# Feed-forward jobs beside attention in one group of sixteen pairs instead of two of eight

## The chip, the cores and the metric

The kernel runs on one core of one Trainium2 chip. The core has a matrix engine (TensorE, PE in the profile, its weight loads PEld), a vector engine (DVE), a scalar engine (ACT), a general one (POOL), and SP, which issues DMAs. Matmuls write to PSUM, eight banks of 128 partitions x 512 f32; ACT and DVE read it from there. The metric is the device time of one execution in microseconds: 1838.07 us as median of three runs before the change (1837.73 to 1839.37).

## What is computed

One transformer block over 2048 tokens of width 512, all in f32: a modulated layer norm, attention with 32 heads of 16, a residual, a second modulated layer norm, a gated feed-forward part of width 1792, a residual.

```python
mod = (_silu(c) @ w_mod).reshape(1, 6, 1, -1)
sa, ca, ga, sb, cb, gb = (mod[:, i] for i in range(6))
h = _layernorm(x) * (1 + ca) + sa
qkv = (h @ wqkv).reshape(B, S, 3, 32, 16)           # q, k, v: [heads, S, 16]
p = _softmax(einsum("bhqd,bhkd->bhqk", q, k) * 16 ** -0.5)
x = x + ga * (einsum("bhqk,bhkd->bhqd", p, v) @ wo)
h = _layernorm(x) * (1 + cb) + sb
x = x + gb * ((_silu(h @ w_gate) * (h @ w_up)) @ w_down)
```

## The kernel before

**Precision.** An f32 product is formed as three products of a high and a low part (terms (0,0), (0,1), (1,0) of hi and lo). Scores are made with 48 rows: 16 head rows in three such combinations stacked on the partitions, two heads of a group on rows 0 to 63 and 64 to 127; two further rows (KR = 48, KR + 1) carry the negated row maximum.

**Units, steps, pairs.** The queries are cut into four chunks of 512 (NC), the heads into eight groups of four (NG). A unit u is one chunk with one group, 32 in all. A unit has 16 steps, one for each 128 keys; a step has four pairs. A pair (`pair_of`) is one score matmul (`score`, L568, 128 keys x 512 queries of one head) on one half of the array's rows, and beside it on the other half one matmul for row maxima (`max_one`, L521), 20 steps ahead (LEAD - 1) of the scores. ACT turns each score bank into exps (L570) in a tile `pt_`, of which there are 13 (PTS). DVE reduces each bank of the maxima (L523). For the last 80 pairs there are no maxima left. `done` counts pairs up to 4n = 2048.

**pv.** `pv_step(i, half)` multiplies the four exp tiles of step i with v, for half the queries: eight PE instructions (L583) of 32 array columns and 256 elements, two quads. They run as four column tiles side by side and add to one bank for the whole unit. Behind the last step ACT copies the bank to o (L587), and `close_unit` issues the DMA of the denominators, the loads of k and q of unit u + 3 and, some steps later through `at`, the reciprocal (L598), the load of the broadcast reciprocals rb, and on POOL o times rb (L610) with its store. `pvs(most, by_halves)` issues up to `most` halves whose step lies at least 8 pairs back (`4 * halves[0][0] + 8 <= done`).

**Two ways to go on.** `plain(steps)` goes in windows of three pairs, each followed by one or two halves of pv, with four banks for maxima (0 to 3), three for scores (4 to 6) and bank 7 for pv. `filled(places, work)` runs feed-forward work beside the pairs: after pair r it takes `places[r]` slots of the work, then come `hook()` and `pvs(6, False)`. The maxima have banks 0, 1, 2 there, the scores 4 and 5, the work accumulates in banks 3 and 6 (`outs`, FBANKS), pv in 7. In the last 80 pairs ALONE replaces the places, and the scores have five banks.

**Feed-forward work.** After a chunk's eight units its output projection (`out_pair`, two jobs of two row tiles), gate and up products (`gate_up`, 14 jobs, f = 0 to 13) and down products (`down`, 14 jobs, two for each m = 0 to 6) run beside the next chunk's attention. In `accumulate` with `halves` a slot is two matmuls of 64 rows, one on each half of the array, one to each of the two `outs`: in phase 0 outs[0] gets the upper 64 rows and outs[1] the lower, in phase 1 the other way round. A `gate_up` or `out_pair` job has 12 slots a phase, 24 in all, a `down` job 6 and 12. The chunk's jobs come in the order gate 0, 1, 2, down (0, 0), (0, 2), gate 3, 4, down (1, 0), (1, 2), and so on to gate 13 and down (6, 0), (6, 2). In the main loop an `out_pair` or `gate_up` job goes in two calls of `filled` with TWO, one phase each, with a block of pv between; a `down` job in one call with DOWN. Between the phases of a `down` job `read_both` lets ACT copy one element of each of the two banks (L878), so that the second phase's matmuls wait until the first phase has landed.

After its last slot a `gate_up` job issues the tanh on ACT (L835), and in `hook` follow q and m32 on DVE (L839, L841) and the split of m32 into `mid` on POOL (L843, L844). A `down` job adds its two banks to x on DVE (L855) right after its last slot. `out_pair` leaves two additions (L803) to `hook` and the sums for the norm (L807, L808) to `side`, from which each pair takes one entry. `max_turned` puts a unit's negated maxima into the rows KR of q: a small reduce m, a scaling on ACT, two small DVE instructions and eight DMAs on SP.

**Order.** All engines run their instructions in the order in which the program issues them (`tc.manual_schedule()`); waits between engines follow from the tiles. `gate_up` asks on SP for the next job's weights (`wgu`, two tiles of 1 MB); `down` for the next `wd` after its second job. The main loop for each of the first three chunks: `plain` up to step STARTS (147, 275, 403), two `out_pair` jobs, `plain(9)`, `plain(3)` with the transposes of the normalised rows, in the third chunk `plain(24)`, then the jobs (all 28, in the third chunk 21; the rest runs after the attention). Before the last couple of down jobs stands `plain(3)`.

Of the kernel before, what the change touches and what calls it, by code (L numbers as in the profile page):

```python
# [19 lines left out]
P = 128  # L20
# [23 lines left out]
PTS = 13  # L44
FBANKS = (3, 6)
# [4 lines left out]
TWO = (0, 3, 2, 2, 2, 2, 1, 0)  # L50
DOWN = (0, 3, 3, 0, 3, 3, 0, 0)
ALONE = {TWO: (0, 4, 0, 4, 0, 4, 0, 0), DOWN: (0, 6, 0, 0, 0, 6, 0, 0)}

# [48 lines left out]
def block_kernel(ctx, tc, x, wqkv, wo, w_gate, w_up, w_down, c, w_mod, out):  # L102
# [391 lines left out]
    posts = []  # L494
    n = 16 * NU
# [66 lines left out]
    def score(i, h):  # L562
        u, kt = divmod(i, 16)
        rows = slice(64 * (h % 2), 64 * (h % 2) + KR + 2)
        p_ = pb.tile([P, CW], F32, name="pt_", tag="pt", bufs=PTS)
        pts.setdefault(i, {})[h] = p_
        sp = bank("st_")
        nc.tensor.matmul(sp, kop[u % 3][rows, h // 2, kt * P:(kt + 1) * P], qop[u][rows, h // 2, :],  # L568
                         start=True, stop=True)
        nc.scalar.activation(p_, sp, AF.Exp, scale=SCALE)  # L570

    def pv_step(i, half):

        u, kt = divmod(i, 16)
        g = u % NG
        cols = slice(half * HQ, (half + 1) * HQ)
        if kt == 0 and half == 0:
            pv[u] = single("pv")
            o_[u] = pf.tile([P, CW], F32, name="o", tag="o", bufs=2)
        p_ = pts.pop(i) if half else pts[i]  # L580
        for h in range(4):
            e0 = (kt * H + 4 * g + h) * (DH + 1)
            nc.tensor.matmul(pv[u][32 * h:32 * h + 32, cols], v_flat[:, e0:e0 + 32], p_[h][:, cols],  # L583
                             start=(kt == 0 and half == 0), stop=(kt == 15),
                             skip_group_check=half == 1)
        if kt == 15 and half:
            nc.scalar.copy(o_[u], pv[u])  # L587
# [19 lines left out]
    def out_c(u, eng, mul, o, rb):  # L607
        ci, g = divmod(u, NG)
        on = pf.tile([P, CW], F32, name="on", tag="on", bufs=1)
        mul.tensor_mul(on, o, rb)  # L610
        eng.dma_start(o_dr[ci, g], on)
# [204 lines left out]
    def out_pair(ch, t0, outs, halves):  # L816
        return accumulate(outs, lambda e, a, k: ch.oT[a][:, k, (t0 + e) * P:(t0 + e + 1) * P],
                          lambda b, k: ch.wo[k // 2][:, b, k % 2, :], NK,
                          lambda: posts.append(lambda: add_o(ch, t0, outs, True)), halves)
# [7 lines left out]
    def gate_up(ch, f, outs, halves):  # L827
# [5 lines left out]
        def after():  # L833
            th = tmp("th")
            nc.scalar.activation(th, outs[0], AF.Tanh, scale=0.5)  # L835

            def later():
# [11 lines left out]
                          halves)  # L849
# [85 lines left out]
    def after(i):  # L935
# [9 lines left out]
        if i == -2:  # L945
# [4 lines left out]
            kop[2] = pf.tile([P, 2, S], F32R, name="kop2")  # L950
            ones_rows(2)
# [44 lines left out]
    def pvs(most, by_halves):  # L996
# [4 lines left out]
        while most and halves and 4 * halves[0][0] + 8 <= done:  # L1001
# [30 lines left out]
    def filled(places, work):  # L1032
# [3 lines left out]
        four, bank = three, Turn(4, 5)  # L1036
        if done >= 4 * n - 4 * (LEAD - 1):
            places, bank = ALONE.get(places, places), Turn(4, 5, 0, 1, 2)
        for r in range(len(places)):
            pair_of()  # L1040
            take(work, places[r])
            if r % 4 == 3:
                end_steps()
        hook()
        pvs(6, False)
# [14 lines left out]
    for ci in range(last):  # L1060
        plain(STARTS[ci] - done // 4)
        ch = chunks[ci]
        for t0 in (0, 2):
            work = out_pair(ch, t0, outs, True)
            filled(TWO, work)
            filled(TWO, work)
# [5 lines left out]
        for _ in range(len(ch.jobs) - (KEEP if ci == last - 1 else 0)):  # L1072
# [3 lines left out]
            work = job(ch, *args, outs, True)  # L1076
            for places in (TWO, TWO) if job is gate_up else (DOWN,):
                filled(places, work)
# [80 lines left out]
```

## Time and profile before

| | us |
|---|---|
| median of three runs | 1838.07 |
| lowest, highest | 1837.73, 1839.37 |
| the profiled execution | 1838.88 |
| its span, first to last instruction | 1837.1 |
| PE busy in it | 1825.5 |
| DVE busy | 1532.5 |
| ACT busy | 1243.7 |
| POOL busy | 460.4 |

The granted clock of TensorE is 1.000 over the whole span. The profile's page gives busy time by engine, and by line with the count, the mean time of one instruction, and the idle time before it with what ended it. PE's matmuls are pipelined, so that a PE that reads as busy can still run at different paces; its pace is read from the starts of its matmuls in the timeline. A row of the timeline gives the start in us from the span's start, the length, the engine, the line, the operation, what it writes and reads, the form, and how many like ones in a row are merged.

### The profile page before, as it was taken

How to read it: one execution, taken by the hardware profiler on the slowest of the kernel's cores; microseconds unless marked ns; L12 is line 12 of the kernel's file. 1: busy time of each engine (PE TensorE's matmuls, PEld its weight loads, DVE VectorE, ACT ScalarE, POOL GpSimd, SP SyncE). 2: the span in 40 equal slices, each digit the busy share in tenths (PEclk: the TensorE clock that was granted, in tenths of full speed). 3: DMA queues.
4: the chain of work that ended last, by engine and by line, in shares of the span. 5: the costliest groups of instructions: out<-in, count | busy, mean ns of one | idle time of the engine just before them, and what ended most of it. 6: DMA issues, size and time to landing. Idle time of an engine off the chain costs nothing.

```text
span 1837.1 us, 41048 instructions
## 1 busy us (share of the span) xinstructions
PE 1825.5 (99%) x16904; PEld 1198.2 (65%) x16904; DVE 1532.5 (83%) x2578; ACT 1243.7 (68%) x2386; POOL 460.4 (25%) x541
## 2 busy tenths in 40 slices
PE   9999999999999999999999999999999999999999
PEld 7876444444455777776565777776564577777887
DVE  5578999999999888889999888889999988831544
ACT  4223888888877777777878777777878877774211
POOL 3612544565223111111123111111123011130200
PEclk9999999999999999999999999999999999999999
DMA  8884876657845444453544554444643545333642
GB/s 305 286 225 149 183 185 199 168 189 178 209 79 125 102 120 141 118 147 70 149 103 105 134 132 116 123 117 90 158 81 57 111 93 149 138 122 121 271 169 110
DMA packets 80488, 267.63 MB, mean 146 GB/s; under 512 B 19604, under 2 KB 24212, under 8 KB 59620
## 3 DMA queue, kind: packets, MB, share of 16 engines
q1 hardware_dynamic: 61324, 179.71, 33.8%
q0 software_dynamic: 18288, 84.49, 19.3%
q8 instruction: 133, 2.18, 0.5%
q10 hardware_dynamic: 688, 0.80, 0.2%
q14 instruction: 55, 0.45, 0.1%
HBM read 201.85 MB, written 62.13 MB: 144 GB/s over the span
## 4 chain that ended last, share of the span: by engine, by line
PE 96%; DVE 2%; ACT 1%; DMA 1%; SPq 0%; issue 0%; DVEq 0%
PE bank L583 27%; PE bank L781 19%; PE bank L568 18%; PE bank L521 14%; PE bank L791 8%; PE bank L211 7%; DVE mx L523 1%; PE bank L824 1%; DMA wm_ab<-in_w_mod 1%; PE bank L765 0%; DVE stt L807 0%; PE bank L533 0%; PE bank L163 0%; PE bank L534 0%; PE bank L535 0%
## 5 line engine op out<-in xcount | busy, mean ns | idle before, releaser
L523 DVE TENSOR_REDUCE mx<-bank 128x1 f32<-128x512 f32 x2048 | 1276.0, 681 | 108.5 <-PE bank L521 66.2
L568 PE MATMUL bank<-qop,kop 50*128 50x512 f32 x2048 | 730.2, 425 | 1.0 <-ACT pt__16517 L570 0.2
L521 PE MATMUL bank<-kop,qop 48*128 48x512 f32 x2048 | 726.6, 425 | 2.9 <-DVE mx L523 2.6
L568 PEld LDWEIGHTS bank<-qop,kop 50*128 50x128 f32 x2048 | 342.6, 184 | 169.9 <-issue 55.6
L521 PEld LDWEIGHTS bank<-kop,qop 48*128 48x128 f32 x2048 | 343.5, 184 | 113.9 <-DVE mx L523 67.7
L781 PE MATMUL bank<-act,wgu 64*128 64x512 f32 x1872 | 300.9, 392 | 0.0
L781 PEld LDWEIGHTS bank<-act,wgu 64*128 64x128 f32 x1872 | 196.1, 187 | 24.7 <-issue 0.2
L610 POOL TENSOR_TENSOR on<-o,rb 128x512 f32<-128x512 f32 x31 | 39.8, 1284 | 498.1 <-DMA rb<-d_dr 363.6
L781 PE MATMUL bank<-wd,mid 64*128 64x512 f32 x912 | 134.0, 397 | 0.0
L843 POOL CAST mid<-m 128x512 fp32r<-128x512 f32 x40 | 24.3, 608 | 379.3 <-DVE m L841 176.5
L781 PEld LDWEIGHTS bank<-wd,mid 64*128 64x128 f32 x912 | 88.0, 185 | 15.9 <-ACT first L878 3.2
L211 PE MATMUL bank<-hT,wqs 128*128 128x512 f32 x384 | 94.3, 397 | 0.4 <-DVE wqs L351 0.4
L839 DVE SCALAR_TENSOR_TENSOR q<-th,bank 128x512 f32<-128x512 f32 x56 | 38.2, 682 | 54.4 <-ACT th L835 54.4
L211 PEld LDWEIGHTS bank<-hT,wqs 128*128 128x128 f32 x384 | 70.7, 188 | 18.8 <-issue 2.9
L835 ACT ACTIVATE th<-bank 128x512 f32<-128x512 f32 x56 | 33.3, 594 | 58.1 <-PE bank L791 58.1
L855 DVE TENSOR_TENSOR x<-bank,x 128x512 f32<-128x512 f32 x84 | 53.9, 685 | 18.3 <-PE bank L781 16.8
L841 DVE TENSOR_TENSOR m<-bank,q 128x512 f32<-128x512 f32 x56 | 38.7, 691 | 21.7 <-PE bank L791 19.7
L844 POOL TENSOR_TENSOR mid<-m,mid 128x512 fp32r<-128x512 f32 x40 | 51.5, 1287 | 3.3
L791 PE MATMUL bank<-wd,mid 128*128 128x512 f32 x216 | 51.4, 393 | 0.0
L211 PE MATMUL bank<-wqs,hT 128*128 128x512 f32 x192 | 48.0, 398 | 0.0
L781 PE MATMUL bank<-wgu,act 64*128 64x512 f32 x288 | 47.8, 394 | 0.1
L791 PEld LDWEIGHTS bank<-wd,mid 128*128 128x128 f32 x216 | 40.3, 188 | 9.1 <-POOL mid L844 0.3
(6298 smaller groups left out, 5133.0 us busy)
## 6 DMA issues: line engine op xcount, KB each, us to landing
wgu<-gu_dr SPq DMA_DIRECT2D x48, 1024.0 KB
wd<-wd_dr SPq DMA_DIRECT2D x28, 1024.0 KB
kop<-kd SPq DMA_DIRECT2D x33, 768.0 KB
kop<-kd POOLq DMA_DIRECT2D x29, 768.0 KB, 8.8
gu_dr<-wgu POOLq DMA_DIRECT2D x14, 1024.0 KB, 13.5
kd<-prt SPq DMA_DIRECT2D x16, 512.0 KB
qd<-prt SPq DMA_DIRECT2D x16, 512.0 KB
kop<-gu_dr SPq DMA_DIRECT2D x8, 1024.0 KB
```

The costliest lines, as they stand in the source:

```text
L211: nc.tensor.matmul(pt, lhs(a, k), rhs(b, k), start=(n == 0), stop=(n == 3 * nk - 1))
L521: nc.tensor.matmul(pm, qop[u][rows, s, qt * P:(qt + 1) * P], kop[u % 3][rows, s, kc * CW:(kc + 1) * CW], start=True, stop=True)
L523: nc.vector.tensor_reduce(mx[u][:, b, s, qt, kc:kc + 1], pm, op=ALU.max, axis=AX.X)
L568: nc.tensor.matmul(sp, kop[u % 3][rows, h // 2, kt * P:(kt + 1) * P], qop[u][rows, h // 2, :], start=True, stop=True)
L583: nc.tensor.matmul(pv[u][32 * h:32 * h + 32, cols], v_flat[:, e0:e0 + 32], p_[h][:, cols], start=(kt == 0 and half == 0), stop=(kt == 15), ...
L610: mul.tensor_mul(on, o, rb)
L781: nc.tensor.matmul(outs[e], lhs(e, a, k)[rows], rhs(b, k)[rows], start=(ph == 0 and j == 0), stop=(j == z and (ph == 1 or trade is not None)),
L791: nc.tensor.matmul(outs[e], lhs(e, a, k), rhs(b, k), start=(j == 0), stop=(j == z))
L839: nc.vector.scalar_tensor_tensor(q, th, 1.0, outs[0], op0=ALU.add, op1=ALU.mult)
L841: nc.vector.tensor_mul(m32, outs[1], q)
L844: (nc.gpsimd if slow else nc.vector).tensor_sub(mid[:, 1, :], m32, mid[:, 0, :].bitcast(F32))
L855: nc.vector.tensor_add(ch.x2[:, t, :], outs[e], ch.x2[:, t, :])
```

## The change

A gate, up or out job now runs in one call of `filled` with FOUR, 16 pairs with 24 slots, and one block of up to ten halves behind it, drawn with a lag of four pairs. As both phases lie in one group, `read_both` stands between them (`trade`). The second down job of a couple has places of its own and the lag of four as well. A group of 16 pairs holds 16 exps, so four exp tiles are added (MORE, in the pool `pf`), the tiles go round in a list (`ring`) that the program keeps itself, and where 17 wouldn't do up to four halves are drawn before a group. Space for the tiles comes from o (one buffer, taken only at the unit's end) and from rb (the product with o is written in place). Where a unit's pv begins beside other work, bank 7 trades places with the next bank of the maxima. The tanh of a gate job moves into `hook`. In the last 80 pairs a FOUR job runs as two groups of eight as before.

```diff
@@ -42,14 +42,15 @@
 ORDER = (0, 2, 1, 3)
 UG = 16 * NG
 PTS = 13
+MORE = 4
 FBANKS = (3, 6)
 KEEP = 7
 REST = 24
 NORM = 9
 STARTS = (147, 275, 403)
-TWO = (0, 3, 2, 2, 2, 2, 1, 0)
-DOWN = (0, 3, 3, 0, 3, 3, 0, 0)
-ALONE = {TWO: (0, 4, 0, 4, 0, 4, 0, 0), DOWN: (0, 6, 0, 0, 0, 6, 0, 0)}
+FOUR = (1, 2, 1, 2, 2, 1, 3, 0, 3, 1, 2, 1, 2, 1, 2, 0)
+DOWN = ((0, 3, 3, 0, 3, 3, 0, 0), (0, 3, 3, 0, 2, 1, 1, 2))
+ALONE = {FOUR: (0, 4, 0, 4, 0, 4, 0, 0), DOWN[0]: (0, 6, 0, 0, 0, 6, 0, 0), DOWN[1]: (0, 6, 0, 0, 0, 6, 0, 0)}
 
 
 def run(it):
@@ -492,6 +493,7 @@
     pf = None
     qop, mx, pts, pv, o_, due, res = {}, {}, {}, {}, {}, {}, {}
     posts = []
+    ring = [pb.tile([P, CW], F32, name=f"pt{k}", bufs=1) for k in range(PTS)]
     n = 16 * NU
     last = NC - 1
 
@@ -562,7 +564,8 @@
     def score(i, h):
         u, kt = divmod(i, 16)
         rows = slice(64 * (h % 2), 64 * (h % 2) + KR + 2)
-        p_ = pb.tile([P, CW], F32, name="pt_", tag="pt", bufs=PTS)
+        p_ = ring.pop(0)
+        ring.append(p_)
         pts.setdefault(i, {})[h] = p_
         sp = bank("st_")
         nc.tensor.matmul(sp, kop[u % 3][rows, h // 2, kt * P:(kt + 1) * P], qop[u][rows, h // 2, :],
@@ -575,8 +578,10 @@
         g = u % NG
         cols = slice(half * HQ, (half + 1) * HQ)
         if kt == 0 and half == 0:
+            if beside and u and done < 4 * n - 4 * (LEAD - 1):
+                j = three.ids[three.n % len(three.ids)]
+                banks[7], banks[j] = banks[j], banks[7]
             pv[u] = single("pv")
-            o_[u] = pf.tile([P, CW], F32, name="o", tag="o", bufs=2)
         p_ = pts.pop(i) if half else pts[i]
         for h in range(4):
             e0 = (kt * H + 4 * g + h) * (DH + 1)
@@ -584,6 +589,7 @@
                              start=(kt == 0 and half == 0), stop=(kt == 15),
                              skip_group_check=half == 1)
         if kt == 15 and half:
+            o_[u] = pf.tile([P, CW], F32, name="o", tag="o", bufs=1)
             nc.scalar.copy(o_[u], pv[u])
 
 
@@ -606,9 +612,8 @@
 
     def out_c(u, eng, mul, o, rb):
         ci, g = divmod(u, NG)
-        on = pf.tile([P, CW], F32, name="on", tag="on", bufs=1)
-        mul.tensor_mul(on, o, rb)
-        eng.dma_start(o_dr[ci, g], on)
+        mul.tensor_mul(rb, o, rb)
+        eng.dma_start(o_dr[ci, g], rb)
 
     def at(i, f):
         due.setdefault(i, []).append(f)
@@ -816,7 +821,7 @@
     def out_pair(ch, t0, outs, halves):
         return accumulate(outs, lambda e, a, k: ch.oT[a][:, k, (t0 + e) * P:(t0 + e + 1) * P],
                           lambda b, k: ch.wo[k // 2][:, b, k % 2, :], NK,
-                          lambda: posts.append(lambda: add_o(ch, t0, outs, True)), halves)
+                          lambda: posts.append(lambda: add_o(ch, t0, outs, True)), halves, trade=halves and read_both)
 
     def out_terms(ch, t, pt, ks):
         for k in ks:
@@ -831,10 +836,15 @@
         ch.mid[f] = mid = tile_mid()
 
         def after():
-            th = tmp("th")
-            nc.scalar.activation(th, outs[0], AF.Tanh, scale=0.5)
-
-            def later():
+            def half():
+                th = tmp("th")
+                nc.scalar.activation(th, outs[0], AF.Tanh, scale=0.5)
+                return th
+
+            th = None if halves else half()
+
+            def later(th=th):
+                th = th or half()
                 q = tmp("q")
                 nc.vector.scalar_tensor_tensor(q, th, 1.0, outs[0], op0=ALU.add, op1=ALU.mult)
                 m32 = tmp("m32")
@@ -846,7 +856,7 @@
 
         w = ch.w.pop(f)
         return accumulate(outs, lambda e, a, k: w[:, 2 * e + a, k, :], lambda b, k: ch.hT[b][:, k, :], NK, after,
-                          halves)
+                          halves, trade=halves and read_both)
 
     def down(ch, m, t0, outs, halves):
         def later():
@@ -948,6 +958,7 @@
             es_a0.close()
             pf = ctx.enter_context(tc.tile_pool(name="pf", bufs=1, side="right", reuse_waits="tile"))
             kop[2] = pf.tile([P, 2, S], F32R, name="kop2")
+            ring[:0] = [pf.tile([P, CW], F32, name=f"pt{PTS + k}") for k in range(MORE)]
             ones_rows(2)
             load_k(2)
             load_q(2)
@@ -993,12 +1004,12 @@
         while side:
             side.pop(0)()
 
-    def pvs(most, by_halves):
+    def pvs(most, by_halves, lag=8):
 
         nonlocal owed
         if by_halves:
             most, owed = most + owed, 0
-        while most and halves and 4 * halves[0][0] + 8 <= done:
+        while most and halves and 4 * halves[0][0] + lag <= done:
             i, half = halves.pop(0)
             pv_step(i, half)
             most -= 1
@@ -1034,15 +1045,23 @@
         nonlocal four, bank, beside
         beside = True
         four, bank = three, Turn(4, 5)
+        lag = 4 if len(places) == 16 or places == DOWN[1] else 8
+        twice = 1
         if done >= 4 * n - 4 * (LEAD - 1):
+            twice, lag = len(places) // 8 or 1, 8
             places, bank = ALONE.get(places, places), Turn(4, 5, 0, 1, 2)
-        for r in range(len(places)):
-            pair_of()
-            take(work, places[r])
-            if r % 4 == 3:
-                end_steps()
-        hook()
-        pvs(6, False)
+        if done - 4 * halves[0][0] + len(places) > PTS + MORE:
+            pvs(4, False, 4)
+        for k in range(twice):
+            if k:
+                bank = Turn(4, 5, 0, 1, 2)
+            for r in range(len(places)):
+                pair_of()
+                take(work, places[r])
+                if r % 4 == 3:
+                    end_steps()
+            hook()
+            pvs(6 if len(places) < 16 else 10, False, lag)
 
     def two_of(u):
         return [kop[u % 3][:, e, :].rearrange("p (k c) -> p k c", k=NK) for e in range(2)]
@@ -1061,9 +1080,7 @@
         plain(STARTS[ci] - done // 4)
         ch = chunks[ci]
         for t0 in (0, 2):
-            work = out_pair(ch, t0, outs, True)
-            filled(TWO, work)
-            filled(TWO, work)
+            filled(FOUR, out_pair(ch, t0, outs, True))
         side.append(lambda: scaled(ch))
         plain(NORM)
         plain(WIN, [lambda tp, k=k: ch.turned(tp, k) for k in range(NK)])
@@ -1073,9 +1090,7 @@
             job, args = ch.jobs.pop(0)
             if args == (NF // FG - 1, 0):
                 plain(WIN)
-            work = job(ch, *args, outs, True)
-            for places in (TWO, TWO) if job is gate_up else (DOWN,):
-                filled(places, work)
+            filled(FOUR if job is gate_up else DOWN[args[1] // 2], job(ch, *args, outs, True))
     chunks[last - 1].load_gu(NF - 2)
     filled((0,) * 4, iter(()))
 
```

## The prediction

> **What bounds the kernel now.** I read the page first, then the groups by line, the busy time of two stretches, and last the timelines of TensorE, VectorE and ScalarE through one stage.
>
> ```profile
> span 1837.1 us, 41048 instructions
> PE 1825.5 (99%) x16904; PEld 1198.2 (65%) x16904; DVE 1532.5 (83%) x2578; ACT 1243.7 (68%) x2386; POOL 460.4 (25%) x541
> L523 DVE TENSOR_REDUCE mx<-bank 128x1 f32<-128x512 f32 x2048 | 1276.0, 681 | 108.5 <-PE bank L521 66.2 <-PE bank L568 34.1
> 300.00:371.40 71.40, 71.40 (x716) 34.41 (x712) 70.73 (x122) 61.54 (x123) 34.88 (x35) 1.00 0.70 194
> 646.90:687.70 40.80, 40.80 (x438) 29.96 (x434) 36.40 (x61) 29.19 (x56) 6.85 (x8) 1.00 0.48 125
> ```
>
> The last two rows give a stretch's length, then the busy time of PE, PEld, DVE, ACT and POOL, each with its instructions. PE reads as busy everywhere, so it doesn't say who bounds. DVE does: in the plain stretch (300 to 371 us) it has work for 70.73 of 71.40 us; beside the other matmuls (646.9 to 687.7 us: four TWO groups and two DOWN groups) it is idle for 4.4 of 40.8 us. So there are two regimes. Plain is paced by the maxima's reduces:
>
> ```profile
> 864.19 0.50 PE L568 MATMUL bank<-qop,kop 50*128 50x512 f32 x1
> 864.76 3.68 DVE L523 TENSOR_REDUCE mx<-bank 128x1 f32<-128x512 f32 x6 [0.20 <-PE bank L568]
> 868.36 0.24 DVE L598 RECIPROCAL dn<-dn 128x16 f32<-128x16 f32 x1
> 868.51 5.63 DVE L523 TENSOR_REDUCE mx<-bank 128x1 f32<-128x512 f32 x9
> 886.05 14.56 DVE L523 TENSOR_REDUCE mx<-bank 128x1 f32<-128x512 f32 x24 [0.25 <-PE bank L521]
> ```
>
> 24 reduces follow each other in 14.56 us, one every (14.56 - 0.69) / 23 = 0.60 us. The first rows are an entry into plain, whose first score starts at 864.19: DVE runs without a gap from the first reduce on.
>
> In the filled groups PE is the bound. One TWO group, from the pv quads before it to the next group:
>
> ```profile
> 700.81 0.38 PE L583 MATMUL bank<-pt__8112,v_flat 128*32 128x256 f32 x1
> 701.14 0.50 PE L568 MATMUL bank<-qop,kop 50*128 50x512 f32 x1
> 701.48 0.39 PE L568 MATMUL bank<-qop,kop 50*128 50x512 f32 x1
> 704.52 0.39 PE L568 MATMUL bank<-qop,kop 50*128 50x512 f32 x1
> 705.69 0.40 PE L521 MATMUL bank<-kop,qop 48*128 48x512 f32 x1
> 706.02 0.40 PE L583 MATMUL bank<-pt__8146,v_flat 128*32 128x256 f32 x1
> 706.26 0.38 PE L583 MATMUL bank<-pt__8146,v_flat 128*32 128x256 f32 x1
> 707.56 0.38 PE L583 MATMUL bank<-pt__8203,v_flat 128*32 128x256 f32 x1
> 707.89 0.50 PE L568 MATMUL bank<-qop,kop 50*128 50x512 f32 x1
> ```
>
> I call a score with its maximum, or the two matmuls of one slot, an item. A group of 8 pairs and 12 slots has 20 items; item 1 starts at 701.48 and item 19, the last pair, at 705.69: 4.21 / 18 = 0.234 us each, pair or slot alike. A half of pv is two quads of 0.217 us ((707.56 - 706.26) / 6), 0.43 us in all. Four steps are longer than that: the first pair takes 0.34 us, the last pair 0.33, the first quad 0.24, the last quad 0.33. Their excess, 0.106 + 0.096 + 0.023 + 0.113 = 0.34 us, is what going from pairs to pv and back costs, once a group of 6.75 us.
>
> **The change part by part.** I count groups from the loops. FOUR runs for 6 out pairs and for gate jobs 0 to 13, 0 to 13 and 0 to 7 of the three chunks: 42 times with maxima. One more starts at pair 1964, four before the maxima end. 15 couples of down jobs run directly behind a FOUR with maxima, two more behind a plain stretch.
>
> 1. **Two groups become one.** 42 changes to pv and back go: -0.34 each.
>
> 2. **The read between the two phases (read_both) is new in FOUR.** In TWO a pv block lay between the phases; now only two pairs do, as in DOWN:
>
> ```profile
> 716.14 0.87 PE L781 MATMUL bank<-wd,mid 64*128 64x512 f32 x6
> 718.08 0.39 PE L568 MATMUL bank<-qop,kop 50*128 50x512 f32 x1
> 722.99 0.87 PE L781 MATMUL bank<-wd,mid 64*128 64x512 f32 x6
> 725.02 0.39 PE L521 MATMUL bank<-kop,qop 48*128 48x512 f32 x1
> 717.03 0.20 ACT L878 COPY first<-bank 1x1 f32<-1x1 f32 x2
> 717.30 0.60 ACT L570 ACTIVATE pt__8409<-bank 128x512 f32<-128x512 f32 x1
> 704.94 0.60 ACT L570 ACTIVATE pt__8248<-bank 128x512 f32<-128x512 f32 x1
> ```
>
> Three slots, two pairs and three slots are 8 items, 1.87 us; they took 1.94 us in the first down group and 2.03 in the second. So the read costs 0.07 to 0.16 us; I take 0.12. FOUR has the same three slots, two pairs there. Bounds: nothing and 0.18. Queued behind the two copies on ACT is one exp (717.30), 0.27 us later than the copies' start; its bank has slack. On PE all of the second phase stands behind the waiting slot. [...]
>
> So a FOUR takes 0.34 + 38 x 0.234 + 0.33 + 0.12 = 9.68 us to its pv and 0.24 + 14 x 0.217 + 0.33 = 3.61 for 16 quads: 13.29 against 13.50. The 42 bring 42 x -0.21 = -9 us.
>
> 3. **Inside the burst.**
>
> ```profile
> 708.46 5.22 DVE L523 TENSOR_REDUCE mx<-bank 128x1 f32<-128x512 f32 x8 [1.52 <-PE bank L568]
> L545 DVE TENSOR_REDUCE m<-mx 128x16 f32<-128x64 f32 x16 | 3.5, 220 | 0.5
> L550 DVE SCALAR_TENSOR_TENSOR parts<-m,parts 128x16 fp32r<-128x16 f32 x16 | 2.6, 165 | 1.0 <-ACT parts L560 1.0
> L552 DVE STREAM_TRANSPOSE turned<-parts 128x32 f32<-128x32 f32 x16 | 3.4, 212 | 0.7 <-DVE parts L550 0.2
> L839 DVE SCALAR_TENSOR_TENSOR q<-th,bank 128x512 f32<-128x512 f32 x56 | 38.2, 682 | 54.4 <-ACT th L835 54.4
> L841 DVE TENSOR_TENSOR m<-bank,q 128x512 f32<-128x512 f32 x56 | 38.7, 691 | 21.7 <-PE bank L791 19.7
> L843 POOL CAST mid<-m 128x512 fp32r<-128x512 f32 x40 | 24.3, 608 | 379.3 <-DVE m L841 176.5 <-PE bank L521 164.4 <-PE bank L568 38.3
> L844 POOL TENSOR_TENSOR mid<-m,mid 128x512 fp32r<-128x512 f32 x40 | 51.5, 1287 | 3.3
> L807 DVE BATCH_NORM_STATS2 stt<-x 128x6 f32<-128x512 f32 x12 | 8.2, 684 | 0.0
> ```
>
> PE asks for 16 maxima in 9.3 us, one every 0.58, with three banks; DVE gives one every 0.60. The first reduce starts 0.57 us after its maximum (707.89 to 708.46). Followed one by one, each 0.60 behind the last or 0.43 behind its own matmul, and freeing its bank 0.74 after its start (0.69 and a release of some 0.05), the reduces let PE pass: with places FOUR the tightest maxima, pairs 3 and 14, come 0.43 us after their bank is free. DVE's side jobs (the 0.24 us reciprocal above, and a unit's m, parts and transpose, 0.22 + 0.17 + 0.21) fall into that 0.43 once a unit; when two meet, 0.1 to 0.2 is lost. I put 0.1 on each of 15 cycles of 48 pairs: +1.5, bounds 0 and 6. Scores have two banks: an exp starts 0.42 us after its score (704.52 to 704.94) and lasts 0.60; same-bank scores in FOUR are at least 5 items (1.17 us) apart, so they pass. Tanh moves behind exp 16 and runs under pv; q and m behind it (0.7 us each) end about 12.3 us into the group, before the next first slot at 13.6; the cover is the eight halves, and without it up to 1.5 us would show. POOL's cast and subtraction of mid (0.61 + 1.29) end about 14.3, with the DMA issues behind them on its queue; the down job that reads this mid comes a whole FOUR later, and wgu is asked for on SP once in 13.3 us as before in 13.5. Nothing is lost there.
>
> 4. **DOWN.** pvs now leaves nothing over at a FOUR's end, so the first down group, still with lag 8, has one step ready: two halves instead of four. The second takes six. No switch is saved, and the DVE cover goes:
>
> ```profile
> 714.63 0.50 PE L568 MATMUL bank<-qop,kop 50*128 50x512 f32 x1
> 721.49 0.49 PE L568 MATMUL bank<-qop,kop 50*128 50x512 f32 x1
> 719.33 1.29 DVE L855 TENSOR_TENSOR x<-bank,x 128x512 f32<-128x512 f32 x2
> 720.53 1.28 DVE L523 TENSOR_REDUCE mx<-bank 128x1 f32<-128x512 f32 x2
> ```
>
> The group took 6.86 us; four quads fewer make it 5.99. Its reduce 6 stands behind two additions to x, runs 720.53 to 721.22 and frees the bank of the next group's second maximum, which PE would start at 714.63 + 5.99 + 0.34 = 720.96. With the release PE waits 0.30 us, and the slots behind that pair with it. Bounds: 0.26, and 0.5 where a unit's m reduce (0.2 us) falls in. In the new second DOWN, pair 7 follows pair 5 after 4 items (0.94 us), but its bank needs 0.42 + 0.60 and the release: 0.09 to 0.25 late, since 705.69 in TWO came 0.15 after its exp's end without waiting; I take 0.15. So 15 x 0.45 + 2 x 0.15 = +7.
>
> 5. **Lag 4 moves pv out of plain.** Before, each filled run handed one step (4 exps) on to the plain stretch behind it. Now it hands on none: FOUR and the second DOWN clear it, and a run's first FOUR draws two halves more at its start (the 17 tiles demand it). Plain leaves one step open as before. So in each of the seven runs that end in plain (three in chunks 0 and 1, the out pairs of chunk 2), two halves of 0.43 us move from where DVE hides them to where PE is the bound: 7 x 0.86 = +6, less about 0.5 for DVE's backlog that they let drain: +5.5. If plain gave the time back it would be 0; the rows from 864.76 say that DVE had no gap there.
>
> 6. **Bank trade, late o, rb in place.** In TWO's grouping a unit ended with its group; now it ends inside, and the trade spares PE the copy of o there. The next maximum on the old bank comes over 2 us later. Nothing, bounds -0.1 and +0.1 a unit (16 units). One rb buffer is reused a unit later; nothing.
>
> 7. **Rest.** The FOUR at pair 1964 now runs its last 12 scores with two banks and singly: +0.4. The sums behind the first out pair (two of 0.68 us on DVE and their aggregates) meet a longer burst: +0.1 in each chunk. Together +0.7.
>
> Sum: -9 + 1.5 + 7 + 5.5 + 0.7 = +5.7. The profiled execution took 1838.88 us (span 1837.1 and 1.8 around it), 0.8 above the median of three, 1838.07. On the median that is 1843.8; I say **1843.5 us**.
>
> **Rivals.** (a) Forecast, 1843.5: chance 0.45. (b) **The read is covered.** If ACT is free earlier in FOUR than in DOWN, the phases join without a wait, 5 us less: 1838.5, no change. For it: ACT is 72% busy there; against: the first copy starts only when the last slot is done. 0.22. (c) **The plain regime and DOWN's second maximum give their time back**, the one mechanism being that DVE is ahead of PE: if reduce 6 of the first DOWN ends before 720.9 on that clock, the 15 x 0.30 go, and if DVE idles at the entry to plain, the 5.5 too: 1843.5 - 4.5 - 5.5 = 1833.5, faster than before. For it: DVE's 4.4 idle microseconds in 40.8; against: the additions' place in the order. 0.20. (d) **The burst falls behind DVE.** If the 0.43 us of slack isn't there, each FOUR is paced by 16 x 0.60 and its side jobs and gives 0.2 back: 42 x 0.2 = 8 more, 1852. It decides once a burst's reduces start more than 0.43 us later than I reckon. 0.13. [...] That the groups don't merge can't be: the places and the loop are plain.
>
> **How the numbers follow.** A measurement tells about 0.2% (3.7 us). Above 1841.7: most of (a) and all of (d), 0.51. Within: (b) and a part of (a), 0.29. Below 1834.4: (c), 0.20. The range goes from 1831, which takes in (c) with a read of 0.07, to 1852, (d).
>
> **What would show it.** FOUR groups of 13.3 us, first pair to first pair; a jump of about 0.1 us before the second phase's slots; down groups of 6.0 and 8.2 us with a wait of 0.3 us before the second's second maximum; the first pv of plain after nine pairs, not six, with DVE still without a gap. FOURs of 13.5 us or more would mean (d); down couples of 13.8 instead of 14.2 would break step 4; plain stretches that get shorter by 0.8 us would break step 5.

## The result and the profile after

| us | before | after |
|---|---|---|
| median | 1838.50 (6 runs) | 1874.38 (6 runs) |
| lowest, highest | 1837.72, 1839.43 | 1868.04, 1877.60 |
| profiled execution, its span | 1838.88, 1837.1 | 1874.98, 1873.2 |
| granted clock of TensorE over the span | 1.000 | 0.989 |

The ratio is 1.019, with a 95% interval of 1.018 to 1.020: slower by 36 us, where 5.7 were predicted. Among the six executions of after the time goes with the clock: the one at 0.993 took 1868.04, the one at 0.986 took 1877.60. One of the eleven executions of a later run, e10, took 2823.33 us at a granted clock of 0.556, and its ratio leaves this slow one out.

The page of after: span, busy time by engine, and the granted clock in 40 slices.

```profile
span 1873.2 us, 41352 instructions
PE 1856.7 (99%) x16904; PEld 1194.7 (64%) x16904; DVE 1518.0 (81%) x2578; ACT 1242.9 (66%) x2476; POOL 459.1 (25%) x541
PEclk9999999999999999999998999999998999999999
```

The matmuls are the same in number, yet PE is 31 us longer busy, and two slices have an 8 in the clock's row. I cut both executions at the starts of the score matmuls, pair by pair (the two programs run the pairs in the same order), and summed the differences:

| stretch | number | before, each | after, each | difference in all |
|---|---|---|---|---|
| 36 pairs of plain behind the out pairs | 3 | 24.31, 24.30, 24.28 | 26.64, 29.59, 29.79 | +13.1 |
| couple of down jobs behind a FOUR | 15 | 13.74 | 14.55 | +12.1 |
| other stretches at a change between plain and filled | 16 | | | +11.9 |
| the other FOURs with maxima | 37 | 13.53 | 13.45 | -3.0 |
| the FOUR at pair 1964, and the part without maxima | 2 | 12.37, 47.19 | 13.46, 48.77 | +2.7 |

Unrounded they add up to 36.9; ahead of the first score and behind the last, after is 0.8 shorter.

The largest line first. The next rows are the busy time of after in stretches behind the second pair of out jobs: length; PE, PEld, DVE, ACT, POOL with their instructions; granted clock, DMA share, GB/s.

```profile
977.70:981.10 3.40, 2.46 (x7) 0.98 (x7) 3.26 (x11) 2.39 (x5) 0.02 (x1) 1.00 0.01 2
981.10:994.70 13.60, 13.07 (x76) 5.56 (x76) 9.35 (x16) 6.98 (x14) 5.78 (x18) 0.50 0.00 1
994.70:1006.00 11.30, 11.16 (x124) 5.24 (x116) 10.47 (x18) 9.73 (x19) 1.19 (x2) 1.00 0.82 123
```

The same place in before, just behind the entry into plain:

```profile
965.30:968.70 3.40, 3.35 (x26) 1.30 (x22) 3.33 (x8) 2.90 (x6) 0.00 (x0) 1.00 0.20 77
```

In 3.4 us after has 7 matmuls, before 26 (a row counts all that run in the stretch, also those begun ahead of it). Then after's clock is 0.50 for 13.7 us. PE's timeline there: start, length, engine, line, operation; in brackets the idle time before it and what ended it.

```profile
978.68 0.50 PE L571 MATMUL bank<-qop,kop 50*128 50x512 f32 x1
980.55 0.49 PE L523 MATMUL bank<-kop,qop 48*128 48x512 f32 x1 [0.89 <-DVE mx L525]
981.63 0.79 PE L523 MATMUL bank<-kop,qop 48*128 48x512 f32 x1 [0.58 <-DVE mx L525]
982.95 1.93 PE L588 MATMUL bank<-pt,v_flat 128*32 128x256 f32 x16
```

The same form of matmul takes 0.49 us, then 0.79: that is how a lower clock looks in rows. Ahead of it PE waits for DVE's reduces. DVE's timeline at the same place behind the first out pairs shows why they come late:

```profile
562.41 0.66 DVE L525 TENSOR_REDUCE mx<-bank 128x1 f32<-128x512 f32 x1
562.99 0.68 DVE L812 BATCH_NORM_STATS2 stt<-x 128x6 f32<-128x512 f32 x1
563.71 0.18 DVE L813 BATCH_NORM_AGGREGATE mv<-stt 128x2 f32<-128x6 f32 x1
563.80 0.66 DVE L525 TENSOR_REDUCE mx<-bank 128x1 f32<-128x512 f32 x1
```

The norm's sums alternate with the reduces, one reduce in 1.39 us instead of 0.60. Before had pv for PE to do there. After comes in with no pv left (lag 4 cleared it), so nine pairs pass before the first pv at 982.95.

Ahead of the last 2 us of the span the clock falls five times, each time behind an entry into plain: at 564.7 us (for 6.8 us), 899.2 (3.4), 981.1 (13.7), 1319.0 (3.4), 1400.9 (13.7). The trace's records of the clock up to there hold 1.000 and 0.500 and nothing between (a row of it with 0.99 reaches a little into a stretch at 0.500). All lengths at 0.500 are 3.4 or a multiple of it, and so are the distances between the starts (from 564.7 to 899.2 are 98 times 3.413 us). PE doesn't stand idle for long ahead of these drops: the longest gap is 0.89 us, and ahead of those at 899.2 and 1319.0 there is none over 0.01. The clock came back after one, two or four times 3.413 us; in the drop at 981.1, one of four, PE was busy for 13.07 of 13.60 us.

**The down couples**, PE's timeline of one (first score of each group, and around the second group's start), and DVE's:

```profile
637.68 0.50 PE L571 MATMUL bank<-qop,kop 50*128 50x512 f32 x1
643.75 0.49 PE L571 MATMUL bank<-qop,kop 50*128 50x512 f32 x1
644.08 0.39 PE L571 MATMUL bank<-qop,kop 50*128 50x512 f32 x1
644.40 0.50 PE L523 MATMUL bank<-kop,qop 48*128 48x512 f32 x1
652.25 0.50 PE L571 MATMUL bank<-qop,kop 50*128 50x512 f32 x1
```

```profile
642.46 1.29 DVE L865 TENSOR_TENSOR x<-bank,x 128x512 f32<-128x512 f32 x2
643.66 6.24 DVE L525 TENSOR_REDUCE mx<-bank 128x1 f32<-128x512 f32 x10
```

The groups take 6.07 and 8.50 us; the means of the 15 couples are 6.05 and 8.50, in before 6.83 and 6.91. The second pair's score starts at 644.08, its maximum at 644.40: 0.32 late. The reduce that frees its bank stands behind the two additions and starts at 643.66.

**A FOUR** in after, PE's timeline:

```profile
665.66 0.50 PE L571 MATMUL bank<-qop,kop 50*128 50x512 f32 x1
668.10 0.50 PE L571 MATMUL bank<-qop,kop 50*128 50x512 f32 x1
669.59 0.94 PE L786 MATMUL bank<-act,wgu 64*128 64x512 f32 x6
671.64 0.39 PE L571 MATMUL bank<-qop,kop 50*128 50x512 f32 x1
679.11 0.49 PE L571 MATMUL bank<-qop,kop 50*128 50x512 f32 x1
```

and the weight load ahead of the score at 668.10:

```profile
668.10 0.18 PEld L571 LDWEIGHTS bank<-qop,kop 50*128 50x128 f32 x1 [0.17 <-ACT pt L573]
```

The group takes 13.45. From 668.10 to 669.59 are six items (1.40), and took 1.49: this score waits for the exp that frees its bank. From 669.59 to 671.64, over the read, are eight items (1.87), and took 2.05: 0.18. Over the 42 FOURs with maxima the medians of these two are 0.09 and 0.16.

### The profile page after: what moved, and what is told of

It reads as the page before. It is cut to its first block, busy times and chain, and to the rows that moved or that the text cites. A ratio compares the mean times of both kernels' runs of the same rounds, so it can differ in the third digit from the quotient of the medians.

```text
span 1873.2 us, 41352 instructions
## 1 busy us (share of the span) xinstructions
PE 1856.7 (99%) x16904; PEld 1194.7 (64%) x16904; DVE 1518.0 (81%) x2578; ACT 1242.9 (66%) x2476; POOL 459.1 (25%) x541
## 4 chain that ended last, share of the span: by engine, by line
PE 94%; DVE 3%; ACT 1%; DMA 1%; issue 0%; SPq 0%; DVEq 0%; ACTq 0%
PE bank L588 26%; PE bank L786 19%; PE bank L571 18%; PE bank L523 14%; PE bank L796 8%; PE bank L212 7%; DVE mx L525 2%; ACT pt L573 1%; PE bank L829 1%; DMA dn<-o 1%; DMA wm_ab<-in_w_mod 0%; PE bank L770 0%; DVE stt L812 0%; PE bank L535 0%; PE bank L164 0%
## 5 line engine op out<-in xcount | busy, mean ns | idle before, releaser
L525 DVE TENSOR_REDUCE mx<-bank 128x1 f32<-128x512 f32 x2048 | 1258.3, 682 | 144.8 <-PE bank L523 83.2
L573 ACT ACTIVATE pt<-bank 128x512 f32<-128x512 f32 x2048 | 1099.9, 599 | 365.4 <-PE bank L523 177.2
L571 PE MATMUL bank<-qop,kop 50*128 50x512 f32 x2048 | 761.5, 436 | 0.8 <-ACT pt L573 0.6
L523 PE MATMUL bank<-kop,qop 48*128 48x512 f32 x2048 | 753.6, 431 | 6.1 <-DVE mx L525 5.7
L588 PE MATMUL bank<-pt,v_flat 128*32 128x256 f32 x8192 | 536.3, 388 | 0.4 <-ACT pt L573 0.2
L523 PEld LDWEIGHTS bank<-kop,qop 48*128 48x128 f32 x2048 | 355.3, 187 | 125.4 <-DVE mx L525 82.5
L588 PEld LDWEIGHTS bank<-pt,v_flat 128*32 128x32 f32 x8192 | 228.1, 110 | 231.1 <-issue 117.5
L786 PE MATMUL bank<-act,wgu 64*128 64x512 f32 x1872 | 317.9, 396 | 0.6 <-DVE m L851 0.3
L786 PE MATMUL bank<-wd,mid 64*128 64x512 f32 x912 | 150.9, 401 | 0.8 <-DVE m L851 0.3
L615 POOL TENSOR_TENSOR rb<-o,rb 128x512 f32<-128x512 f32 x31 | 39.8, 1285 | 438.9 <-DMA rb<-d_dr 366.4
```

Source lines behind the costliest of these rows:

```text
L523: nc.tensor.matmul(pm, qop[u][rows, s, qt * P:(qt + 1) * P], kop[u % 3][rows, s, kc * CW:(kc + 1) * CW], start=True, stop=True)
L525: nc.vector.tensor_reduce(mx[u][:, b, s, qt, kc:kc + 1], pm, op=ALU.max, axis=AX.X)
L615: mul.tensor_mul(rb, o, rb)
L786: nc.tensor.matmul(outs[e], lhs(e, a, k)[rows], rhs(b, k)[rows], start=(ph == 0 and j == 0), stop=(j == z and (ph == 1 or trade is not None)),
```

## The experiments

They came in four groups, e1 to e4, e5 to e7, e8 and e9, and e10, each on one chip beside runs of before (medians 1838.74, 1838.39, 1838.71, 1838.67).

**e1_hand_on**: the last group ahead of each plain hands a step on again.

```diff
-        lag = 4 if len(places) == 16 or places == DOWN[1] else 8
+        lag = 4 if not keep and (len(places) == 16 or places == DOWN[1]) else 8
...
+            filled(FOUR, out_pair(ch, t0, outs, True), t0 == 2)
...
+            filled(..., args in ((NF - 1,), (NF // FG - 1, 2)))
```

> The changed kernel, but the last group ahead of each plain stretch keeps lag 8 and so hands one step of pv on to plain, as before. Clock theory (plain entered with nothing left of pv runs nine pairs with no pv between, PE does too little there and the granted clock falls to 0.5): the clock is 1.000 over the whole span, the stretch behind the out pairs takes 24.3 us again instead of 26.6 to 29.8, the seven entries together give back about 20 us, 1855. Rival (the clock falls because of the longer pv blocks or bursts of the groups, which stay): the mean clock stays at 0.99 and only the moved halves come back, about 6 us, 1868. Third reading (neither; the waits in the down couples are all): within 2 us of 1874.

Measured: 1853.29 (1852.14 to 1855.85), ratio 1.0076 (1.0061 to 1.0091), 21 us less than after. The clock stays at 1.000 in the profiled execution. The busy time of the 3.4 us behind the entry into plain:

```profile
968.90:972.30 3.40, 3.35 (x20) 1.64 (x20) 2.73 (x6) 2.83 (x6) 0.53 (x1) 1.00 0.20 77
```

20 matmuls instead of 7, and the 36 pairs take 24.30, 24.32 and 24.30 us again. By stages 15 to 16 of the 21 us are the clock (13.1 behind the out pairs, the rest behind the last couples); 5.6 are the step itself: second out jobs 2.3, gate 13 jobs 1.7, last couples 2.2 shorter, the short plains 0.7 longer.

**e2_twice**: after, but PE gets more to do: in the first nine pairs of a plain behind filled groups the matmul for the maxima is issued twice into the same bank.

```diff
+        if again:
+            nc.tensor.matmul(pm, ..., start=True, stop=True)
         nc.tensor.matmul(pm, ...
...
+            again = fresh and w < 3
```

> The changed kernel, in which the first nine pairs of each plain stretch behind a filled group issue their maxima's matmul twice; nothing is taken away. Clock theory: more work on PE where VectorE sets the pace keeps the granted clock at 1.000; PE's 9 x 0.23 us more are hidden behind the reduces, and the time falls by 14 to 18 us, to 1857 to 1860. Rival (pv halves or waits are what costs at the entries): the clock makes no difference there, PE has more to do, so the time is the same or up to 7 x 2 us longer, 1874 to 1888.

Measured: 1872.77 (1871.79 to 1873.72), ratio 1.0180 (1.0165 to 1.0195). Not the 1857 to 1860 that the clock theory gave: behind the last couples the clock held, behind the out pairs it fell all the same (6.8, 6.8 and 13.7 us). The busy time there:

```profile
977.90:981.30 3.40, 2.20 (x11) 1.07 (x10) 3.30 (x10) 1.66 (x4) 0.82 (x5) 0.99 0.00 0
981.30:988.10 6.80, 6.80 (x40) 2.81 (x38) 4.16 (x8) 3.02 (x7) 4.99 (x14) 0.50 0.00 0
```

DVE sets so slow a pace there that twice the maxima make 11 matmuls. The run left open whether the theory was wrong or the dose too small.

**e3_before_hold** asks from the other side: before, with nothing added; the two halves of pv of plain's second window are held to the third, so that nine pairs pass without pv.

```diff
+            more = (0, -HALVES[3], HALVES[3])[w] if fresh and w < 3 else 0
-            pvs((HALVES[(w - 2) % 4] if done > 8 else 0) + (w == 4 * steps // WIN - 1), True)
+            pvs((HALVES[(w - 2) % 4] if done > 8 else 0) + more + (w == 4 * steps // WIN - 1), True)
```

> The kernel before, in which plain behind a filled group holds the two halves of its second window back to the third; nothing is added or left out. Clock theory: the nine pairs without pv are enough by themselves, the granted clock falls as in the changed kernel, mean 0.99, and the time grows by 12 to 20 us, to 1850 to 1858. Rival (it needs the larger groups): the clock stays at 1.000 and, as VectorE sets the pace there, the time stays within 2 us of 1838.

Measured: 1851.86 (1850.96 to 1853.04), ratio 1.0065 (1.0048 to 1.0082), as the clock theory had it. A delay of two halves by three pairs makes before 13 us slower, and the clock falls at the same five places (6.8, 3.4, 3.4, 3.4, 6.8 us). Its busy time:

```profile
972.40:975.80 3.40, 1.86 (x8) 0.70 (x8) 3.26 (x11) 2.32 (x5) 0.45 (x3) 1.00 0.00 0
975.80:979.20 3.40, 3.40 (x26) 1.70 (x30) 3.00 (x6) 1.21 (x4) 2.39 (x13) 0.50 0.02 5
```

Before as it is isn't far from this edge. The profiled execution keeps 1.000, but of the 15 executions beside e5 to e7 one shows 0.996 and took 1842.42, where the median is 1838.39.

**e4_down**: after, both down jobs with the old places and lag 4.

```diff
-DOWN = ((0, 3, 3, 0, 3, 3, 0, 0), (0, 3, 3, 0, 2, 1, 1, 2))
+DOWN = ((0, 3, 3, 0, 3, 3, 0, 0), (0, 3, 3, 0, 3, 3, 0, 0))
...
-        lag = 4 if len(places) == 16 or places == DOWN[1] else 8
+        lag = 4
```

> The changed kernel, but both down groups of a couple have the places of the kernel before and lag 4, so that each draws four halves. If the couple's 0.8 us come from the first group's short pv (the second's second maximum waits for VectorE) and from the 4 items between pairs 5 and 7 of the new places, a couple takes 13.8 us instead of 14.55, the 15 couples and the two behind plain give back 12 us: 1862. If lag 4 itself costs (the last step's exps are not ready when pv draws them), couples stay at 14.3 or more and the time within 4 us of 1874.

Measured: 1864.47 (1860.02 to 1865.75), ratio 1.0130 (1.0114 to 1.0147). The median lies between the two readings. The clock still falls (0.991). Couples take 14.12 instead of 14.55, not 13.8: the second group's second maximum is 0.01 late instead of 0.3, and that group reaches its pv after 5.05 instead of 5.78. But a block of four halves, from its first matmul's start to its last's, now takes 1.70 instead of before's 1.56, in both groups. So 0.3 of the 0.38 over before come with lag 4 itself: the block draws the last step, and in the couple at 640.5 us, where the last exp ends at 646.58, one column of the quads starts 0.16 behind the other three from then on.

**e5_four**: e2 with a larger dose, the matmul four times behind the out pairs and twice behind the couples and the last gate jobs.

```diff
+        for _ in range(again):
+            nc.tensor.matmul(pm, ..., start=True, stop=True)
...
+            again = (3 if steps == NORM else 1) * (fresh and w < 3)
```

> The changed kernel, in which the first nine pairs of plain behind the out pairs issue their maxima's matmul four times and those behind the down couples twice; nothing is taken away. Twofold work kept the clock only behind the down couples; behind the out pairs, where VectorE has the sums as well and a pair comes only every 1.1 us, it left PE streaming for about 0.4 of the time and the clock still fell. Clock theory, with a bound between 0.4 and 0.6 of the time: fourfold is 0.8 there, the clock stays at 1.000 over the span, the stretch behind the out pairs takes 24.3 to 26 us instead of 26.6 to 30, and the whole 1857 to 1861, faster by adding work. Rival (not the amount of streaming counts, but that no pv, with its column tiles, runs): the clock falls as before, and the time is 1872 or more.

Measured: 1868.06 (1863.94 to 1868.72), ratio 1.0154 (1.0140 to 1.0168); clock 0.996 to 1.000. Matmuls added, 6 us gained: added work alone could only cost time, and the clock is what changed for the better. The rival, that pv has to run for the clock to stay, fell: behind the second and third out pairs it stayed at 1.000 through nine pairs without pv. The 1857 to 1861 were missed by the price of the added matmuls (36 pairs now 25.65 and 25.70 at full clock) and, in the profiled run, one drop left of 3.4 us and one behind a wait for wgu. The same place as above:

```profile
978.30:981.70 3.40, 3.21 (x18) 2.16 (x17) 3.30 (x9) 2.05 (x4) 1.07 (x6) 1.00 0.00 0
```

18 matmuls and no drop here. In after, ahead of its drop at 899.2, there were 18 also:

```profile
895.80:899.20 3.40, 3.40 (x18) 1.59 (x14) 3.29 (x6) 3.33 (x7) 0.00 (x0) 0.99 0.21 83
899.20:902.60 3.40, 3.40 (x24) 1.47 (x23) 2.37 (x5) 1.41 (x4) 1.17 (x2) 0.50 0.74 140
```

So in these rows 7 to 11 matmuls in the 3.4 us lose the clock, 20 and 26 keep it, and 18 do either. The expectation's bound, 0.4 to 0.6 of the time, was the author's estimate; no run shows its upper end. Twenty in a row is no safe number either; ahead of e3's drop at 893.9:

```profile
890.50:893.90 3.40, 3.40 (x20) 1.62 (x24) 3.40 (x7) 3.40 (x8) 0.59 (x1) 0.99 0.07 22
```

Counted by their starts, matmuls of any form alike, the traces separate better. The twelve kernels' traces, cut between the first score and the last into stretches of 3.413 us in phase with the drops, give 5297 stretches at full clock. All 15 with 14 starts or fewer were followed by a drop, 7 of the 48 with 15 to 19, and none with 20 or more. PE's busy column doesn't tell: it is 3.40 of 3.40 ahead of the drop at 899.2.

**e6_lags**: the lags set anew. A FOUR ahead of a down couple or of plain has lag 8, so that the first down group draws four halves; the second has the old places, lag 4, and 8 ahead of plain; the FOUR at pair 1964 is split where the maxima end.

```diff
+        if split:
+            twice, lag, places = 2, 8, (0, 3, 2, 2, 2, 2, 1, 0)
...
+            filled(FOUR if job is gate_up else DOWN[0], job(...), 8 if hand_on else 4)
```

> The changed kernel with its lags set anew: FOUR keeps lag 8 ahead of a down couple and ahead of plain, so that the first down group draws four halves again and plain gets a step; the second down group has the old places and lag 4, ahead of plain lag 8; the FOUR in which the maxima end runs as a TWO group and one of eight scores with five banks. If clock, down couples and that FOUR are all that the change cost, it loses those 34 us and keeps the 0.07 us a FOUR: 1837 to 1841, a tie with before. If something else of the change costs (ring, bank trade, rb in place), it stays at 1845 or above. If FOUR was worth the 0.21 us that I gave it, 1832 or below.

Measured: 1842.57 (1840.17 to 1844.61), ratio 1.0021 (1.0012 to 1.0030), clock 0.997 to 1.000. Beside before, a pair of gate jobs is 1.0 us shorter and the couple behind it 0.95 longer (a step moved from one to the other): together nothing, where after has +0.7. The part without maxima is 3.5 us longer.

**e7_no_trade**: e1 without the trade of banks.

```diff
-            if beside and u and done < 4 * n - 4 * (LEAD - 1):
-                j = three.ids[three.n % len(three.ids)]
-                banks[7], banks[j] = banks[j], banks[7]
```

> As the run that hands one step on to plain (1853.3 us, clock 1.000), but bank 7 and the maxima's bank no longer trade places where a unit's pv begins. If the trade spares PE the wait for the copy of o inside a pv block (0.43 us to its start, 0.59 long, so about 1.1 us a unit, 16 units or so, of which two thirds end inside a block), the time grows by 8 to 18 us, to 1861 to 1871. If nothing waits there anyway, it stays within 3 us of 1853.

Measured: 1864.45 (1861.25 to 1867.41), ratio 1.0136 (1.0120 to 1.0153), 11 us over e1. The waits between 615 and 640 us (time in all, times, longest):

```profile
PEld bank L585 <- ACT o L590: 1.2, 1, 1.2
```

pv of a new unit waits for the copy of the last one's o. Pairs of gate jobs in which a unit ends take 27.8 to 27.9 us instead of 26.9. About 2 of the 11 us are a drop of the clock behind the first out pairs, although this kernel hands the step on.

**e8_best**: e6 with the first job of each run of FOURs as two groups of eight, so that nothing is drawn at the entry, and lag 8 for the last FOUR with maxima.

```diff
+        if split or two:
+            twice, places = 2, TWO
...
+            hand_on = ... args[0] in (NF - 1, 7 if ci == last - 1 else NF - 1) ...
...
+            pvs(6 if len(places) < 16 else 10, False, 8 if two and k == 0 else lag)
```

> The run with its lags set anew (1842.6 us, span of the profiled execution 1839.0), with two more things put back: each filled run begins with a job in two TWO groups, so that no halves are drawn at its start behind exps that were only just issued (0.38 us each, six entries, 2.3 us); and the last gate job with maxima keeps lag 8, so that units again end where their group's pv ends in the part without maxima, where the banks don't trade (2.65 us there). If the ledger of stages is right, it comes out 4 to 5 us lower: span 1834 to 1835, time 1836 to 1839, a tie with before or 0.1% better, by what 36 FOUR groups gain at 0.07 us each. If it stays at 1842 or above, the ledger misses something.

Measured: 1842.95 (1841.45 to 1845.78), ratio 1.0024 (1.0015 to 1.0033); a miss, 1836 to 1839 were expected. The draws at the six entries went (6.5 us less than e6 there), and the jobs behind them took 6.7 us more. The part without maxima stayed at +3.7, so the lag of the last gate job with maxima wasn't its cause.

**e9_places**: e1 with the old places in the second down group, lag 4 kept.

```diff
-DOWN = (..., (0, 3, 3, 0, 2, 1, 1, 2))
+DOWN = (..., (0, 3, 3, 0, 3, 3, 0, 0))
```

> The run that hands one step on to plain (1853.3 us), with the old places in the second down group and lag 4 kept. If the new places (4 items between pairs 5 and 7, two slots behind the last pair) cost what the wait for VectorE leaves over, a couple goes from 14.55 to 14.2 us and the time falls by 5 to 7 us, to 1847. If only the wait for VectorE (0.30 us) counts, the couple stays at 14.5 and the time within 2 us of 1853.

Measured: 1850.63 (1846.08 to 1851.25), ratio 1.0056 (1.0040 to 1.0071), less gained than expected: against e1 the profiled execution lost 4 us ahead of the first filled group, which this run doesn't touch. Couples take 14.16 instead of 14.55, as expected; the new places cost 0.4 each, and 0.4 stay (0.31 of them the wait for the second maximum).

**e10_tanh**: e6, and the tanh right behind its last slot again where no maxima are left. The trace of e6 gave the reason; ACT's timeline and the waits of that stage:

```profile
1645.85 2.19 ACT L573 ACTIVATE pt<-bank 128x512 f32<-128x512 f32 x4 [0.15 <-PE bank L571]
1647.92 0.60 ACT L841 ACTIVATE th<-bank 128x512 f32<-128x512 f32 x1
```

```profile
PEld bank L786 <- DVE m L851: 1.8, 3, 0.6
PEld bank L571 <- ACT th L841: 1.2, 3, 0.4
PEld bank L786 <- DVE q L849: 0.5, 1, 0.5
```

In the hook tanh stands behind four exps, and the next job's slots and scores wait for it and for q and m behind it.

```diff
-            th = None if halves else half()
+            th = None if halves and done < 4 * n - 4 * (LEAD - 1) else half()
```

> The run with its lags set anew (1842.6 us), with the tanh of a gate job issued again right behind its last slot in the part without maxima, elsewhere still in hook. There the scores have five banks, so up to five exps stand on ACT ahead of a tanh in hook; three groups behind gate jobs take 7.0 us instead of 5.8, and their slots wait for q and m. If that is the tanh's place, these groups are back at 5.8 and the time falls by 3.5 us, to 1839, a tie with before. If the bank of pv waits there (a unit's end inside a block), they stay at 7.0 and the time at 1842.

Measured: median 1839.54 (ten of its eleven executions 1837.32 to 1842.22), ratio 1.0005 (0.9996 to 1.0014): a tie with before. The part without maxima is 0.2 over before instead of 3.5, and of the three kinds of wait above none is left. No kernel of this study beat before.

## Why the prediction was right and wrong, step by step

The direction came true, the size didn't. It wasn't luck alone: e1, which keeps the clock, is still 15 us slower than before. The 36 us, from the ledger and the runs: about 15 the clock, 6 the step not handed on, 12 the 15 couples, 2.4 draws at the entries (6.3 in e1, less the 3.9 that come back at the ends of the runs; e8 shows that nothing is won by moving them into the jobs), 2.7 the end of the maxima, 1 the couples behind a plain stretch, and -3 the FOURs.

- **Step 5 failed, and cost most of the miss.** It priced what the moved step adds to the filled groups, and that was right: 5.5 predicted, 5.6 measured by e1. But it treated plain as a stretch that simply keeps its pace. The sign was written down, "the first pv of plain after nine pairs, not six, with DVE still without a gap", and read as harmless. Its first half came true, its second didn't: in the 13.6 us at half clock DVE had work for 9.35. Nine pairs at DVE's pace leave PE with so little to do that its clock halves (7 matmuls in 3.4 us, then 0.50). e1 (clock back), e3 (the same drops in before, by a delay alone) and e5 (more work, less time) show it. No rival named it, although the clock of 1.000 over the whole span was a state that could be lost. The 2.4 us of the draws at the entries weren't in the sum either.
- **Steps 1 and 2, -0.21 a FOUR:** -0.08 came. The changes to pv and back did go; the read cost 0.18 in the group above (the bound) and 0.16 as the median, not 0.12, and a score's wait for its exp took 0.09. Step 3 had called five items between scores on one bank enough (1.17 us); at this place they aren't. With both, 13.29 + 0.06 + 0.09 = 13.44, and the group above took 13.45.
- **Step 3, +1.5 for the burst:** the reduces kept up, as predicted; rival (d) didn't come. "Nothing is lost there" was wrong for tanh where no maxima are left: e10 against e6 shows the mechanism, 3.3 us there. In after this part is 1.6 us longer, and its tanh wasn't run by itself.
- **Step 4, DOWN:** the mechanism was right, the size off. First group 6.07 (predicted 5.99), wait for the second maximum 0.32 (predicted 0.30), but the new places cost 0.4 (e9), not 0.15, and 0.1 more comes over the read of the first group (from its fifth score to its sixth 1.11 us instead of before's 1.02): +0.8 a couple instead of +0.45, 12 us instead of 7. e6 gives the first group its four halves back and has the old places as e9 has; over the gate jobs and these couples it is 4.9 us under e9, 0.33 a couple. So the cover was worth what step 4 said.
- **Step 6, the trade: nothing.** What it was for is right: without it PE waits 1.2 us for the copy of o (e7). That the trade itself, the late o and rb in place cost nothing was not run one by one; e10, which has all three, ties with before.
- **Step 7, +0.7:** the FOUR at pair 1964 alone cost 1.1.
- **Rivals:** (b) fell, the read isn't covered; (c) fell, couples and entries gave nothing back; (d) fell, FOURs took 13.45 on the mean. The range was too narrow because the price of a fallen clock wasn't in any case. (The sum on the median is 1843.8; that 1843.5 was said instead has no reason in the working and doesn't matter here.)

Left open: why the clock came back after 3.4, 6.8 or 13.7 us, what decides with 15 to 19 starts, and why the first down group's read got 0.1 us longer.

## What to carry to other kernels

Hidden work had two uses here: it cost little where DVE set the pace (handing the step on to plain took 6.2 us off the filled groups in e1 and put 0.7 on the short plains), and it kept TensorE busy there (26 matmuls in 3.4 us and a clock of 1.000 with it, 7 and then 0.50 without). Before moving such work out, count the matmuls that are left in each 3.4 us of that stretch, from their starts and not from PE's busy time or its idle gaps; if few are left (here 14 or fewer were followed by a drop every time, 15 to 19 in 7 of 48 stretches), the clock may fall as it did here, to 0.50, and even added matmuls can pay (6 us in e5). And putting an instruction later on an engine's queue can cost time in a stage in which that engine is behind: the tanh behind four exps, 3.3 us (e10 against e6).

## What the runs showed of the hardware that was not expected

- The clock fell to 0.50 without a PE gap over 0.89 us, for 3.4, 6.8 or 13.7 us; the same matmul then took 0.79 us instead of 0.49. Delaying two halves of pv by three pairs was enough for 13 us (e3), and no stretch of 3.413 us with 20 or more matmul starts was followed by a drop.
- Four times the maxima's matmuls behind the out pairs, and twice behind the other entries, made the changed kernel 6 us faster (e5).
- Removing a change between two array tilings, worth 0.34 us by its four long steps, brought 0.08, because the one group has a read (0.16 us) and a score's wait (0.09) that the two groups didn't have.
